# Batch 0 of a gated attention and mixer kernel: later score panels, pairwise side blocks, strips two outputs ahead and a later turn of z

## The chip, the cores and the metric

The kernel runs on one core of a Trainium2 chip. The metric is the device time of one execution in microseconds (us); the kernel before has a median of 1001.98 us over 5 runs (998.73 to 1006.83). Engines are named as in the profile: PE (matrix multiply; PEld is its weight load), DVE (vector), ACT (scalar, activations), POOL and SP. POOL and SP do almost nothing here but issue DMAs: POOL the loads and stores, SP the transposing DMAs.

## The reference

For each of 8 batches, with sequence length S = 3136, width 256 and z of width 64:

```
scores = z @ z.T / S                  # (S, S), symmetric
attn   = maximum(scores, 0) ** 2
x      = u * (attn @ v)
h      = (x.T @ U @ V).T              # low rank, 32
x2     = x + h
out    = x2 + maximum(x2 @ w1, 0) @ w2
```

This document is about the first two products in batch 0: the scores, and attn @ v.

## The kernel before

The sequence is cut into 25 tiles of 128 rows, called 0 to 24 (the last, 24, has 64 rows). Since the scores are symmetric, only one of the blocks (j, o) and (o, j) is computed. Panel j, the tile A[j], holds the 13 blocks (j, j) to (j, j+12), counted modulo 25. A score step (`score`, L292 to L314) makes up to 1024 columns of one panel, or a piece each of two: two PE matmuls into a pair of PSUM banks (L298, two such pairs exist), then ACT (relu and scale, L311) into A, then a square in place on DVE (L313). A whole panel of 13 blocks takes two such steps of 832 columns.

Output tile o is the sum over all 25 tiles j of block (j, o) times v[j] (`half`, L371: two matmuls per j on the two halves of the rows). For the 13 tiles j = o-12 to o the block is read from A[j]. For the other 12 the transposed blocks of panel o are needed: one transposing DMA from SP (`turn`, L331 to L334) writes them into a strip. A strip can be made only when the whole panel o is squared, and there are five strip buffers. Outputs are closed in pairs (`close_pair`, L385 to L395: ACT copy, DVE add, DVE multiply by u). Output 24 has 64 rows and works on quarters of the array (L405).

The outputs are taken in the order 12, 13, ..., 24, 0, ..., 11; position i in this order is output (12 + i) mod 25. The order of the instructions on every engine is written by hand: `manual_schedule` keeps program order on each engine, and `_spread` and `_merge` mix two lists of steps evenly.

In batch 0 nothing is there yet, so `start_up` works in groups of outputs. Outputs 12 to 15 are made first, then 16 to 19, which is where the change begins:

- The main part of 16 to 19 runs over pairs of panels; `make_stored` makes, for two panels at once, just the blocks that these four outputs need. Turns of panels 16 to 19 are behind it on SP. In the second and third round stood `double_z(1, ...)` (four DVE copies, L188) and `turn_z(1, ...)` (two transposing DMAs of SP, L195), which turn batch 1's z.
- The tail is the strip part of 16 to 19, merged with score steps: panels 20, 21 and 22 whole (`more`; two steps of panel 20 are taken already before), and the rest of the panels 15 down to 8, one step for each panel (`rest`), up to the panel's end.
- The main loop over i goes on with i = 8, output 20. `attend_steps` gives the 25 steps of an output, and `fill` the score steps spread among them: `first_at` says which panels and side blocks of batch 0 (side blocks are the first columns of panels 3 to 11) are made at which i, `next_at` those of batch 1. After each output, strips are turned four positions ahead: 21 and 22 are turned in the tail, 23 after output 20, 24 and 0 after 21, 1 after 22, and so on. `extend_z(1)` (a DVE copy of the turned z, L238) stands at i = 11. POOL loads two tiles of u for each pair of outputs and one part of v at i = 9, 11, 13, 15, 18 and 21.

From batch 1 on, the loop also has the mixer's matmuls of the batch before; nothing of that changes.

Of the kernel before, what the change touches and what calls it, by code (L numbers as in the profile page):

```python
# [42 lines left out]
def kernel(  # L43
# [31 lines left out]
    NG = 4  # L75
# [216 lines left out]
    def score(b, parts):  # L292

        ps = pair_psum()
        zT = zT_of(b)
        zT_flat = zT.rearrange("p t c -> p (t c)")
        for k, (j, c, n, _) in enumerate(parts):
            mm(  # L298
                out=ps[:, k, :n],
                lhsT=zT[halves[k], j, :],  # L300
                rhs=zT_flat[halves[k], c : c + n],
                start=True,
                stop=True,
            )
        if parts[0][3] is parts[-1][3]:
            n = parts[0][2]
            todo = [(parts[0][3], ps[:, :, :n] if len(parts) == 2 else ps[:, 0, :n])]
        else:
            todo = [(part[3], ps[:, k, : part[2]]) for k, part in enumerate(parts)]
        for dst, src in todo:  # L310
            nc.scalar.activation(out=dst, in_=src, func=AF.Relu, scale=sc)  # L311
        for dst, _ in todo:
            nc.vector.tensor_tensor(out=dst, in0=dst, in1=dst, op=ALU.mult)  # L313
# [345 lines left out]
    def beside(o, j, w, stop=(False, False)):  # L659
        t0, _ = pair_of(o)  # L660
        for h in range(1 if j == NF else 2):
            half(0, o, j, h, w, (t0, h) not in begun, stop[h], skip_group_check=True)
            begun.add((t0, h))

    def start_up():
        parts = ((8, 16), (0, 8), (16, NF))
        first_z(parts[:2])
# [89 lines left out]
                    if 0 <= o - j <= HALF:  # L757
                        beside(o, j, block(0, o, j))

        def make_stored(pair):  # L760
            todo = []
            for j in pair:
                k0, k1 = LEAD - j, min(NB, LEAD + NG - j)
                todo.append((j, LEAD * P, (k1 - k0) * P, A[j][:, k0 * P : k1 * P]))
            score(0, todo)

        nxt += [lambda pair=pair: make_stored(pair) for pair in pairs[:2]]
        run(nxt[:2])
        own = [
            lambda j=j, some=some: use_stored([j], some)  # L770
# [2 lines left out]
            if j <= some[-1]  # L773
        ]
        run(_merge(nxt[2:], own))
        rest = []
        for j in reversed(range(FIRST - NG, LEAD)):
            rest += score_steps(0, j, LEAD + NG - j, NB)
        more = [s for j in range(LEAD + NG, LEAD + 2 * NG - 1) for s in score_steps(0, j)]
        for i, pair in enumerate(pairs):  # L780
            if i + 2 < len(pairs):
                make_stored(pairs[i + 2])
            else:
                more.pop(0)()
            use_stored(pair, outs)
            if B > 1 and i in (1, 2):
                part = ((0, FIRST), (FIRST, NF))[i - 1]
                double_z(1, (part,))
                turn_z(1, (part,))
            if i == len(pairs) - 1:  # L790
                turn(0, LEAD + NG)
        tail = []
        for o in outs:
            js = [(o + 1 + i) % NT for i in range(HALF)]

            def close(o=o, j=js[-1]):
                beside(o, j, block(0, o, j), [o % 2 == 1] * 2)
                if o % 2:
                    close_pair(0, o)
                if o == outs[1]:  # L800
                    load_u(0, LEAD + NG)
                if o < outs[-2]:
                    turn(0, o + NG + 1)

            for i in range(3):
                some = js[4 * i : min(4 * i + 4, HALF - 1)]
                tail.append(lambda o=o, js=some: [beside(o, j, block(0, o, j)) for j in js])
            tail.append(close)
# [8 lines left out]
    for j, i in enumerate((6, 7, 8, 9, 3, 5, 4, 2, 9, 8, 7, 6)):  # L817
        own_at[i].append((j, 0, FIRST - j))

    first_at = {8: [(NT - 2, 0, NB), (0, 0, NB)], 9: [(NT - 1, 0, NB)], 10: [(1, 0, NB)]}  # L820
    first_at.update({11: [(2, 0, NB)], 12: []})
    for j, i in zip(range(3, FIRST), (10, 11, 11, 12, 12, 12, 12, 12, 12)):
        first_at[i].append((j, 0, FIRST - j))
    first_turns = {8: (NT - 2,), 9: (NT - 1, 0)}

    next_at = {i: [] for i in range(NT)}
    for j in range(FIRST):
        next_at[max(NB, FIRST + j)].append((j, FIRST - j, NB))
    for j, i in enumerate((14, 15, 16, 18, 19, 20, 24)):
        next_at[i].append((FIRST + j, 0, NB))  # L830

    def run(steps):
        for s in steps:
# [6 lines left out]
    for b in range(B):  # L840
# [104 lines left out]
```

## Time and profile before

| | |
|---|---|
| median of 5 runs | 1001.98 us (998.73 to 1006.83) |
| the profiled execution, its own time | 1004.27 us |
| its span, first to last instruction | 1002.5 us |
| mean granted TensorE clock | 0.998 |
| PE busy | 984.7 us, 98% |
| ACT busy | 612.6 us, 61% |
| DVE busy | 551.0 us, 55% |
| POOL busy | 171.6 us, 17% |
| turns of strips (SP) | 196 |

The profile is of one execution. A row of a group shows how many instructions it has, their mean duration, and the idle time of the engine ahead of them with what ended it. A PE that is "busy" need not be at its peak: a matmul of 256 columns is shown with about 270 ns from start to end, while the next can start about 54 ns after it. A window's row gives, for a stretch of time, each engine's busy us and the granted clock (1.00 is full speed). The chain of waits goes back from the last instruction to what released it, so it says which engine or DMA set the time at each moment. Waits of SP's queue, which the page does not list, are in an answer of their own.

### The profile page before, as it was taken

To read this page: it belongs to the slowest core of one execution; us is meant where nothing else is said; L and a number is where in the kernel's file an instruction comes from. 1 tells how busy PE (TensorE), PEld (TensorE's weight loads), DVE (VectorE), ACT (ScalarE), POOL (GpSimd) and SP (SyncE) were. 2 spreads that over 40 slices of the span, in tenths; PEclk is the share of its full clock that TensorE was granted. 3 is DMA by queue.
4 is the path that set the end of the run, shared out by engine and by line. 5 is a ranking of instruction groups with operands and counts; after the bars stand their busy time and mean duration, and the time that the engine had idled before them with its cause. 6 is when DMAs were issued, how large, how long until landed. Compare 5 with 4: busy or idle time off the path is not lost.

```text
span 1002.5 us, 31020 instructions
## 1 busy us (share of the span) xinstructions
PE 984.7 (98%) x13688; PEld 777.0 (78%) x13688; DVE 551.0 (55%) x1003; ACT 612.6 (61%) x835; POOL 171.6 (17%) x317
## 2 busy tenths in 40 slices
PE   8899999999999999999999999999999999999998
PEld 5578778787778878788787887778878788787866
DVE  6868754467544665446644566445664457542352
ACT  7877764667646776456764667556674666643154
POOL 5112112111121111221112211122111120011000
PEclk9999999999999999999999999999999999999999
DMA  9999989999899998999999997979989998678633
GB/s 192 185 188 201 179 152 181 193 178 173 149 171 184 175 157 175 186 181 171 162 177 171 182 170 149 186 167 179 173 149 194 168 190 157 123 147 164 128 95 101
DMA packets 414790, 167.94 MB, mean 168 GB/s; under 512 B 389488, under 2 KB 399408, under 8 KB 414656
## 3 DMA queue, kind: packets, MB, share of 16 engines
q1 hardware_dynamic: 385424, 99.68, 62.2%
q0 software_dynamic: 29232, 66.28, 29.0%
q8 instruction: 107, 1.75, 0.7%
q14 instruction: 27, 0.22, 0.1%
HBM read 61.88 MB, written 25.69 MB: 87 GB/s over the span
## 4 chain that ended last, share of the span: by engine, by line
PE 88%; DVE 4%; DMA 4%; ACT 3%; issue 1%; POOL 0%; DVEq 0%; POOLq 0%; ACTq 0%
PE ps L371 46%; PE ps L563 16%; PE ps L610 16%; PE ps L298 6%; ACT A L311 3%; DMA out_dram<-o_sb 2%; DVE A L313 1%; PE ps L405 1%; DMA strip<-A 1%; PE ps L531 1%; DVE x_bf L545 1%; DMA z_c<-in_z_dram 1%; PE ps L479 1%; DVE both L386 1%; DVE x_bf L395 0%
## 5 line engine op out<-in xcount | busy, mean ns | idle before, releaser
L311 ACT ACTIVATE A<-ps 128x832 bf16<-128x832 f32 (+9 forms) x477 | 359.1, 769 | 156.3 <-PE ps L298 147.5
L371 PE MATMUL ps<-v,A 64*128 64x256 bf16 x4988 | 341.8, 269 | 4.9 <-DVE o_sb L624 3.6
L313 DVE TENSOR_TENSOR A<-A 128x832 bf16<-128x832 bf16 (+9 forms) x477 | 244.6, 527 | 133.0 <-ACT A L311 129.8
L371 PE MATMUL ps<-v,strip 64*128 64x256 bf16 x4420 | 308.1, 270 | 2.8 <-DMA strip<-A 2.8
L371 PEld LDWEIGHTS <-A 64*128 64x128 bf16 x4988 | 246.5, 94 | 49.0 <-issue 13.5
L581 ACT ACTIVATE relu_bf<-ps 128x1024 bf16<-128x1024 f32 (+2 forms) x206 | 186.4, 912 | 140.0 <-PE ps L563 139.9
L371 PEld LDWEIGHTS <-strip 64*128 64x128 bf16 x4420 | 222.6, 94 | 37.2 <-DMA strip<-A 3.6
L624 DVE TENSOR_TENSOR o_sb<-ps,x_bf 128x512 f32<-128x512 f32 (+2 forms) x105 | 69.9, 665 | 248.4 <-PE ps L610 217.6
L610 PE MATMUL ps<-w_bf,relu_bf 128*128 128x256 bf16 (+1 forms) x1600 | 201.2, 273 | 0.0
L563 PE MATMUL ps<-ut,w_bf 128*128 128x512 bf16 (+2 forms) x896 | 198.6, 353 | 0.0
L610 PEld LDWEIGHTS <-relu_bf 128*128 128x128 bf16 (+1 forms) x1600 | 152.9, 98 | 45.6 <-issue 3.6
L563 PEld LDWEIGHTS <-w_bf 128*128 128x128 bf16 x896 | 84.8, 98 | 62.1 <-issue 6.9
L355 POOL DMA_DIRECT2D u_sb<-in_u_dram x96 | 53.8, 561 | 455.6 <-DVE x_bf L395 445.9
L298 PE MATMUL ps<-zT 64*128 64x416 bf16 (+8 forms) x812 | 131.6, 312 | 0.0
L385 ACT COPY both<-ps 128x512 f32<-128x512 f32 (+1 forms) x104 | 58.8, 566 | 75.9 <-PE ps L371 69.8
L637 POOL DMA_DIRECT2D out_dram<-o_sb x84 | 46.0, 547 | 281.1 <-DVE o_sb L624 277.8
L386 DVE TENSOR_TENSOR both<-ps,both 128x512 f32<-128x512 f32 (+1 forms) x104 | 69.3, 667 | 28.5 <-ACT both L385 28.0
L395 DVE TENSOR_TENSOR x_bf<-both,u_sb 128x512 bf16<-128x512 f32 (+1 forms) x104 | 69.8, 672 | 3.6
L545 DVE TENSOR_TENSOR x_bf<-ps,x_bf 128x512 bf16<-128x512 f32 (+1 forms) x112 | 65.5, 626 | 7.5 <-PE ps L531 7.4
L298 PEld LDWEIGHTS <-zT 64*128 64x128 bf16 x812 | 43.1, 94 | 4.0
L244 POOL DMA_DIRECT2D v<-in_v_dram x61 | 33.7, 554 | 0.8 <-DMA w_bf<-in_moe_w_ch_dram 0.7
L298 PE MATMUL ps<-relu_bf 64*128 64x416 bf16 (+9 forms) x121 | 22.2, 339 | 4.3 <-ACT A L311 3.2
(54 smaller groups left out, 206.3 us busy)
## 6 DMA issues: line engine op xcount, KB each, us to landing
u_sb<-in_u_dram POOLq DMA_DIRECT2D x96, 256.0 KB, 4.1
out_dram<-o_sb POOLq DMA_DIRECT2D x84, 256.0 KB, 3.2
v<-in_v_dram POOLq DMA_DIRECT2D x57, 192.0 KB, 4.7
strip<-A SPq DMA_TRANSPOSE x196, 5.4
out_dram<-o_sb SPq DMA_DIRECT2D x11, 256.0 KB, 2.0
z_c<-in_z_dram POOLq DMA_DIRECT2D x7, 384.0 KB, 5.7
u_sb<-in_u_dram POOLq DMA_DIRECT2D x16, 64.0 KB, 2.2
ut<-x_bf SPq DMA_TRANSPOSE x56, 3.8
```

Source lines behind the costliest of these rows:

```text
L298: mm(out=ps[:, k, :n], lhsT=zT[halves[k], j, :], rhs=zT_flat[halves[k], c : c + n], start=True, stop=True,)
L311: nc.scalar.activation(out=dst, in_=src, func=AF.Relu, scale=sc)
L313: nc.vector.tensor_tensor(out=dst, in0=dst, in1=dst, op=ALU.mult)
L371: mm(out=acc[t0][h][:, (o - t0) * D : (o - t0 + 1) * D], lhsT=w[halves[h]], rhs=v_both[b % 2][halves[h], j, :], start=start, stop=stop, **kw,)
L385: nc.scalar.copy(out=both[:, :w], in_=banks[1][:, :w])
L386: nc.vector.tensor_tensor(out=both[:, :w], in0=banks[0][:, :w], in1=both[:, :w], op=ALU.add)
L395: nc.vector.tensor_tensor(out=x_at(b, t0, n), in0=split(both[:, :w]), in1=u_sb[:, :n, :].rearrange("p t (a c) -> p t a c", c=P), op=ALU.mult,)
L545: nc.vector.tensor_tensor(out=q, in0=split(ps[h][:, : len(ks) * D]), in1=q, op=ALU.add)
L563: mm(out=ps[i][:, :w] if apart else ps[:, i, :w], lhsT=w1_bf[:, db, (hp + i) * P : (hp + i + 1) * P], rhs=uT[c][:, db, len(chunks[c]) * P ...
L581: nc.scalar.activation(out=relus[c][:, hp : hp + 2, :w], in_=ps[:, :, :w], func=AF.Relu)
L610: mm(out=ps[r, k * D : (k + 1) * D], lhsT=relus[c][:, ht, q : q + (TAIL if two else P)], rhs=w2_bf[:, ht, :], start=(ht < 1 + two), stop=( ...
L624: nc.vector.tensor_tensor(out=o_sb[:p].rearrange("p t (a c) -> p t a c", c=P), in0=split(ps[:p, k0 * D : (k + 1) * D]), in1=x_at(b, t, nk) ...
```

## The change

The change touches batch 0 (and the places where batch 1's first scores are made during batch 0):

- Panels 15 to 8 are no longer completed one by one. `make_stored` is now given the first output, and makes for pairs (15, 14), (13, 12), (11, 10), (9, 8) the blocks for outputs 20 to 23 in the tail. What is left of 15, 14 and of 13, 12 (ten blocks, for outputs 24 on) is made at i = 9 and i = 10.
- Panel 22 leaves the tail for i = 8. Panels 23, 24, 0, 1, 2 follow one for each output, at i = 9 to 13, and side blocks at 10 to 14.
- Strips are turned two outputs ahead: 21 in the tail, 22 after output 20, 23 after 21, 24 after 22, 0 after 23, 1 after 24, 2 and 3 after output 0, 4 and 5 after output 1; from then on four ahead as before.
- `double_z(1)` moves to i = 9, the two turns of z to i = 10 and i = 11, `extend_z(1)` to i = 12.
- Batch 1's first panels are made at i = 16, 17, 18, 20, 21, 22, 24 instead of 14, 15, 16, 18, 19, 20, 24, and its first side block at i = 14 instead of 13.

On SP's queue the two turns of z stood between strips 19 and 20; now the first stands between strips 23 and 24 and the second between 24 and 0. ACT and DVE have four more instructions each, PE eight fewer rows; POOL's order is the same.

```diff
+    def make_stored(pair, first, n=NG):
+        todo = []
+        for j in pair:
+            k0, k1 = first - j, min(NB, first + n - j)
+            todo.append((j, first * P, (k1 - k0) * P, A[j][:, k0 * P : k1 * P]))
+        score(0, todo)
...
-        rest = []
-        for j in reversed(range(FIRST - NG, LEAD)):
-            rest += score_steps(0, j, LEAD + NG - j, NB)
-        more = [s for j in range(LEAD + NG, LEAD + 2 * NG - 1) for s in score_steps(0, j)]
+        rest = [
+            lambda pair=pair: make_stored(pair, LEAD + NG)
+            for pair in zip(range(LEAD - 1, FIRST - NG, -2), range(LEAD - 2, FIRST - NG - 1, -2))
+        ]
+        more = [s for j in (LEAD + NG, LEAD + NG + 1) for s in score_steps(0, j)]
...
-            if B > 1 and i in (1, 2):
-                part = ((0, FIRST), (FIRST, NF))[i - 1]
-                double_z(1, (part,))
-                turn_z(1, (part,))
...
-                if o < outs[-2]:
-                    turn(0, o + NG + 1)
+                    turn(0, LEAD + NG + 1)
...
-    first_at = {8: [(NT - 2, 0, NB), (0, 0, NB)], 9: [(NT - 1, 0, NB)], 10: [(1, 0, NB)]}
-    first_at.update({11: [(2, 0, NB)], 12: []})
-    for j, i in zip(range(3, FIRST), (10, 11, 11, 12, 12, 12, 12, 12, 12)):
+    first_at = {8 + n: [(t, 0, NB)] for n, t in enumerate((22, 23, 24, 0, 1, 2))}
+    first_at[14] = []
+    for j, i in zip(range(3, FIRST), (10, 11, 12, 13, 14, 14, 14, 14, 14)):
         first_at[i].append((j, 0, FIRST - j))
-    first_turns = {8: (NT - 2,), 9: (NT - 1, 0)}
+    first_more = {9: (LEAD - 1, LEAD - 2), 10: (LEAD - 3, LEAD - 4)}
+    first_turns = {8: (22,), 9: (23,), 10: (24,), 11: (0,), 12: (1,), 13: (2, 3), 14: (4, 5)}
...
+    after_first = {i: [] for i in range(NT)}
+    for j in range(FIRST):
+        after_first[max(NB + 1, FIRST + j)].append((j, FIRST - j, NB))
+    for j, i in enumerate((16, 17, 18, 20, 21, 22, 24)):
+        after_first[i].append((FIRST + j, 0, NB))
...
+            if b == 0 and i in first_more:
+                fill.append(lambda pair=first_more[i]: make_stored(pair, LEAD + 2 * NG))
             if more:
-                fill += [s for key in next_at[i] for s in score_steps(b + 1, *key)]
+                coming = next_at if b else after_first
+                fill += [s for key in coming[i] for s in score_steps(b + 1, *key)]
...
-                if b and i == 7:
+                if b == 0 and i == 9:
+                    double_z(b + 1, ((FIRST, NF), (0, FIRST)))
+                if i == (7 if b else 10):
                     turn_z(b + 1, ((FIRST, NF),))
-                if b and i == 10:
+                if i == (10 if b else 11):
                     turn_z(b + 1, ((0, FIRST),))
...
-                if i == 11:
+                if i == (11 if b else 12):
                     extend_z(b + 1)
```

More of the change, by code (lines that the diff above doesn't have):

```diff
@@ L758, in use_stored @@
                         beside(o, j, block(0, o, j))
[L760 to L767, printed above, removed]
+        nxt += [lambda pair=pair: make_stored(pair, LEAD) for pair in pairs[:2]]
         run(nxt[:2])
@@ L775, in start_up @@
         run(_merge(nxt[2:], own))
-        rest = []
-        for j in reversed(range(FIRST - NG, LEAD)):
-            rest += score_steps(0, j, LEAD + NG - j, NB)
-        more = [s for j in range(LEAD + NG, LEAD + 2 * NG - 1) for s in score_steps(0, j)]
+        rest = [
[3 more added lines that the diff above has]
+        more = [s for j in (LEAD + NG, LEAD + NG + 1) for s in score_steps(0, j)]
         for i, pair in enumerate(pairs):
             if i + 2 < len(pairs):
-                make_stored(pairs[i + 2])
+                make_stored(pairs[i + 2], LEAD)
             else:
```

## The prediction, on record before the result

> **What bounds the kernel now.** I read the page's busy times and chain first, then the same sums by stage over the first 73 us (the rest of the order is untouched), then the chain, SP's queue and the waits there.
>
> ```profile
> PE 984.7 (98%) x13688; PEld 777.0 (78%) x13688; DVE 551.0 (55%) x1003; ACT 612.6 (61%) x835; POOL 171.6 (17%) x317
> ...
> PE 88%; DVE 4%; DMA 4%; ACT 3%; issue 1%; POOL 0%; DVEq 0%; POOLq 0%; ACTq 0%
> ```
>
> TensorE carries the run; what is not PE's own in the chain is 12%, part of it at the start. The change removes almost no PE work, so its gain can only be PE waiting, in the stages it touches. Busy us by stage (PE, weight load, DVE, ACT, POOL), then granted clock:
>
> ```profile
> 36.30:44.80 8.50, 7.83 (x115) 5.88 (x117) 6.41 (x12) 7.72 (x13) 0.54 (x1) 1.00 1.29 199
> 44.80:49.20 4.40, 2.05 (x39) 1.70 (x35) 3.36 (x9) 2.63 (x5) 1.07 (x2) 1.00 1.01 240
> 49.20:52.80 3.60, 3.60 (x34) 2.37 (x36) 0.59 (x1) 1.73 (x2) 0.00 (x0) 0.53 1.04 177
> 52.80:62.30 9.50, 9.50 (x164) 7.74 (x160) 6.55 (x12) 7.57 (x11) 1.62 (x3) 1.00 0.93 171
> 62.30:66.50 4.20, 3.64 (x63) 1.76 (x61) 3.94 (x8) 4.11 (x9) 1.03 (x2) 1.00 1.26 126
> 66.50:72.30 5.80, 5.80 (x108) 5.05 (x108) 3.39 (x11) 3.15 (x9) 1.61 (x3) 1.00 1.34 260
> ```
>
> The first row is the strip part of outputs 16 to 19, then come output 20 up to its strip, a stretch at half clock, outputs 20 to 23, output 24 (the short one), and 0 and 1 of batch 0. ACT is full in the first row and in output 24; PE waits in the second. The chain there (start, us, what) and PE's own timeline:
>
> ```profile
> 30.54 5.71 DMA strip<-A
> ...
> 37.88 2.85 ACT A L311 x4
> ...
> 42.95 6.20 DMA strip<-A
> 49.20 0.71 PE ps L371 x6
> ```
> ```profile
> 46.31 0.53 PE L371 MATMUL ps<-v,A 64*128 64x256 bf16 x6
> 49.20 0.71 PE L371 MATMUL ps<-v,strip 64*128 64x256 bf16 x6 [2.35 <-DMA strip<-A]
> ```
>
> PE has used its A blocks of output 20 and waits 2.35 us for strip 20, issued at 42.95. Panel 20's last ACT ends at 36.34. Why so late: SP's queue.
>
> ```profile
> 39.54 3.32 SPq L195 DMA_TRANSPOSE zT<-z_bf  x2
> 42.95 3.06 SPq L333 DMA_TRANSPOSE strip<-A  x1
> ```
>
> Both turns of batch 1's z stand in front of it.
>
> **Gains.** Unit prices from the chain after 68 us: 16 attention matmuls 0.87 us (0.0544 each), a score step of two 416-column matmuls 0.18. An 832-wide ACT takes 0.87, its DVE square 0.59.
>
> (1) Strip 20 takes z's place in SP's queue: issue 39.54, 3.4 us earlier. z's two turns there landed in 4.3 and 5.7 us; so strip 20 is there at 43.8 to 45.2. It is wanted at about 44.4. The wait of 2.35 goes; at most 0.8 of it stays.
>
> (2) The half clock goes with it: 3.6 us at 0.53 cost 3.6 x 0.47 = 1.7. The Trainium skill ("TensorE: Matmul & The Clock Gate", Part 1) puts the fall to half after an idle window of about 3.4 us; here an idle of 2.35 was enough, with the clock at 0.53 right behind it. By the rule new waits of 2 us would be free of it; by the row they may cost 1.7. I go by the row for waits of 2.3 and over.
>
> (3) Tail of outputs 16 to 19 (36.3 to 44.8). PE work: 92 matmuls 5.0 + score steps 1.7 = 6.7 of 8.5 us; 1.8 is lost to ACT, which runs its 12 panel pieces and 2 copies without a pause. Panel 22 (2 x 0.87) and ten blocks of panels 12 to 15 leave. ACT then has 2 x 0.87 + 5 x 0.65 + 0.50 + 0.38 + 0.28 + 2 x 0.59 = 7.3 raw; the old list is 10.0 raw in 8.65 us, so 7.3 takes 6.3. PE has 5.0 + 0.36 + 0.8 = 6.2, and strips 16 to 19 land as before (a wait of 0.4 for strip 17). The loss falls from 1.8 to 0.4: 1.4. Tail ends near 42.9.
>
> (4) Output 24, 62.3 to 66.5: 49 quarter matmuls take 1.33 us in every later batch, six score steps (1344 columns) 0.6; 2.3 of 4.2 is lost to ACT and to changing between the two kinds. Now three score steps stand there, panel 1's two and side 5: I leave 0.5. Gain 1.8.
>
> Sum: 2.35 + 1.7 + 1.4 + 1.8 = 7.2.
>
> **New waits.** Strips come two outputs ahead instead of four. Each output is 2.6 us of matmuls plus its score steps, about 3.2; a strip is wanted halfway into its output. So the lead from the turn to the need is 4.2 us for strip 22 (its panel is squared 0.8 after output 20 ends), 4.9 for 23, 4.2 for 24 (before the short output), 3.9 for 0, about 5 for 1. What a turn takes in this stretch, and over the whole run (min, median, max us from issue to landing):
>
> ```profile
> DMA to landing us min/median/max: 3.7/6.2/8.5
> ```
> ```profile
> DMA to landing us min/median/max: 3.6/5.4/10.4
> ```
>
> The skill's "DMA: Bandwidth & Descriptors", Latency and other measured facts, gives a transposing DMA 261 GB/s: 393 KB in 1.5 us, an estimate by which every lead is ample and the gain is all 7.2. The rows say 5.4 to 6.2, because copies (u 256 KB, v 192 KB) and earlier turns share the engines. I go by 5.4: in before this stretch carried a backlog of turns, which is gone in after.
>
> z's turns are not free where they now stand: the first is queued behind strip 23 and ahead of strip 24, the second ahead of strip 0; each holds SP 1.4 to 1.8 us. Late by: strip 22 0 (its queue is empty) to 1.2; strip 23 0.5; strip 24 5.4 + 1.5 - 4.2 = 2.7, less the 0.5 waited for 23, so 2.2; strip 0 then 5.4 + 1.5 - 3.9 - 2.2 = 0.8. Sum 3.5, between 1.0 (3.7 us a turn) and 13 (8.5 us a turn).
>
> A second new wait: the copy that extends z (L238) stands on DVE at output 24 and needs the second z turn, issued only about 55.5, landing near 61; before it found z landed. Behind it on DVE: the squares of panel 1 and side 5, then the closing of output 24; ACT's two copies L391 wait for that closing, and behind them stand panel 2's pieces, so PE runs out of score PSUM in output 0. ACT comes free near 61 + 0.55 + 1.18 + 0.63 + 0.42 = 63.8, by when PE, held by strips 24 and 0, is at about the same place: 0 beyond the strips' own, with bounds 0 and 1.6. If the strips are on time it is this that costs 1.6.
>
> Half clock for a gap of 2.2: 0 taken, 1.7 the other end.
>
> Free: the four z copies on DVE (1.9 us) at output 21, where DVE has 6.55 of 9.5 busy, cost panel 23's turn 0.6, inside the 0.5 to 1.2 above. Four more ACT and DVE pieces (0.3 to 0.65): ACT in output 22 has 4.2 against PE's 3.5; the two score PSUM pairs carry 1.7. Panels of batch 1 made two outputs later: at outputs 8 to 10 of the batch ACT gets a panel (1.7) beside a side (1.4) in about 3.3 us, hidden; bare, 0.3. POOL's order is unchanged, its loads follow the closings. Side blocks 7 to 11 all in output 1: six to eight small ACTs, 0.3.
>
> Net: 7.2 - 3.5 - 0.3 = 3.4. The profiled execution took 1004.27 around a span of 1002.5: span 999.1. It was 2.3 above the median, so from 1001.98: 998.6.
>
> **Rivals.**
> A. *Turns keep up.* With 3.7 us a turn, as one had in this stretch with an empty queue: late 1.0, and at most 0.6 of the DVE wait: gain 5.6 to 7.2, 995.5. For it: panels 22 on are turned singly, not in a burst. Against: u and v loads fall between them as before.
> B. *One wait for another.* Turns at 6.2, the stretch's median: 0.8 for 22, 1.0 for 23, 2.7 for 24, 0.8 for 0, one fall of the clock 1.7: 7.0. Gain about 0, 1002.
> C. *Slower: a two-output lead shorter than the DMA.* At 8.5 us a turn, the stretch's maximum: strip 22 late 4.3, 24 late 5.8, 1 late 3.3, two falls of the clock 3.4: 16.8 against 7.2, so 1011.5. It decides from about 6.3 us a turn. For it: in before the turns issued while a u and a v load were in flight took 7 to 8.5. Against: strip 24's queue holds one z turn and one short load.
>
> **How the numbers follow.** Forecast (gain 2 to 5.2) 0.45; A 0.25; B (-2.5 to 2) 0.16; C 0.14. 0.5% (5 us) is about what a measurement of this kernel tells from no change. Faster by more: A and a third of the forecast, 0.39. Slower by more: C, 0.14. Within: 0.47. The range from 994 (all 7.2, plus run to run) to 1004.5 (B's far end) leaves out C and the best edge of A, 0.2.
>
> **What would show it.** Step 1 and 2: no PE wait for a strip between 43 and 46, clock 1.00 throughout. Step 3: ACT with pauses in the tail, output 20 begins near 42.9. Step 4: quarter matmuls within 2.5 us. New waits: PE waits for strips at outputs 24 and 0, of 2.2 and 0.8; DVE waits for a DMA before L238. Batch 0's output 1 ends at 72.3 before, near 69 after. I am wrong if turns after 46 us take under 4 or over 7 us, or if PE falls to half clock again.

## The result, and the profile after

The changed kernel takes 1006.20 us in the median of 43 runs (1003.25 to 1012.98), beside 1002.61 for the kernel before in 80 runs (998.73 to 1010.82) on the same chips. The ratio is 1.0038, 95% interval 1.0029 to 1.0048: 3.8 us slower (the two medians lie 3.6 apart), certain in sign, and within the 0.5% that the prediction called no change. The forecast was 998.6 with a range up to 1004.5; the time lies above both.

The profiled execution of after took 1007.02 us, with a span of 1005.1 (before: 1004.27 and 1002.5). The page of after, the same two lines as shown of before:

```profile
PE 984.9 (98%) x13684; PEld 778.6 (77%) x13684; DVE 552.2 (55%) x1007; ACT 612.6 (61%) x839; POOL 171.1 (17%) x317
...
PE 87%; DMA 6%; DVE 4%; ACT 2%; issue 0%; POOL 0%; DVEq 0%; POOLq 0%; ACTq 0%
```

No engine has more work worth naming (DVE 1.2 us). In the chain, DMA went from 4% to 6% of the span, and ACT from 3% to 2%: TensorE waits for transfers instead of for ACT. By stage, with the columns as in the prediction (stretch, busy us of PE, weight load, DVE, ACT and POOL, granted clock, DMA share, GB/s), but cut where after's own outputs begin and end:

```profile
36.70:43.20 6.50, 6.46 (x109) 5.55 (x110) 4.12 (x8) 4.89 (x9) 0.00 (x0) 1.00 1.21 227
43.20:46.20 3.00, 2.86 (x46) 2.06 (x42) 2.96 (x9) 1.97 (x6) 0.54 (x1) 1.00 1.27 171
46.20:52.90 6.70, 5.86 (x98) 4.88 (x92) 5.82 (x13) 5.78 (x9) 1.07 (x2) 1.00 0.95 131
52.90:59.30 6.40, 5.62 (x92) 4.38 (x92) 3.09 (x8) 3.99 (x7) 1.62 (x3) 1.00 1.18 173
59.30:66.50 7.20, 3.29 (x48) 1.48 (x47) 2.73 (x5) 2.96 (x5) 1.08 (x2) 0.71 1.24 192
66.50:72.30 5.80, 5.80 (x77) 4.27 (x77) 4.39 (x10) 4.45 (x9) 1.09 (x2) 0.77 0.75 162
```

The tail of 16 to 19 (first row) is short and full of PE, output 20 is at its strip by 45.1, at full clock: the first half of the forecast came true. The row of output 24 (59.3 to 66.5) is where it is lost: PE is busy 3.29 of 7.20 us, and the clock falls there and in the row after. TensorE's timeline of after, where it begins on strips 20, 22, 24 and 2 (in brackets the idle time ahead):

```profile
45.14 0.83 PE L371 MATMUL ps<-v,strip 64*128 64x256 bf16 x12
...
53.68 0.72 PE L371 MATMUL ps<-v,strip 64*128 64x256 bf16 x10 [1.41 <-DMA strip<-A]
...
64.24 1.07 PE L405 MATMUL ps<-v,strip 64*64 64x256 bf16 x16 [3.91 <-DMA strip<-A]
...
77.78 0.28 PE L371 MATMUL ps<-v,strip 64*128 64x256 bf16 x2 [1.80 <-DMA strip<-A]
```

Strip 20 no longer makes it wait; 22, 24 and 2 do, 7.1 us together. The chain of after shows the same three as transfers (start, us, what):

```profile
38.88 6.22 DMA strip<-A
...
47.75 5.89 DMA strip<-A
...
55.38 8.81 DMA strip<-A
...
71.37 6.37 DMA strip<-A
```

SP's queue at the two turns ahead of output 24:

```profile
53.30 1.96 SPq L195 DMA_TRANSPOSE zT<-z_bf  x1
55.38 4.53 SPq L333 DMA_TRANSPOSE strip<-A  x1
```

Strip 24 is issued at 55.38 and wanted at 60.3, where PE has nothing else left: a lead of 4.9 us, against 8.8 from issue to landing. DVE at that place:

```profile
65.76 0.56 DVE L238 COPY zT<-zT 128x1536 bf16<-128x1536 bf16 x1 [4.12 <-DMA zT<-z_bf]
```

The extension of z stood 4.1 us for its turn, and everything behind it on DVE with it. The prediction had such a wait, but with its end near 61.

A useful ruler is the start of the multiply that closes each pair of outputs (L395), after minus before, in the profiled runs: -0.9 and -1.2 us at (16,17) and (18,19), **-5.4 at (20,21)**, -3.5 at (22,23), +0.8 at 24, **+5.2 at (0,1)**, +5.4 at the end of batch 0 and until 263 us. So the change is 5.4 us ahead there, and between 52 and 80 us loses nearly 11. Some 0.6 of the 5.4 is score work that it only puts off past output 21 (an estimate from the matmul columns of L298 made by then, at 0.0544 us for 256: 8.4 us before, 7.8 after); by the end of batch 0 both have made the same. It ends at +2.6, mostly because two PE waits of 2.0 and 1.7 us for DVE's work in the mixer at 283 and 649 us, in before's profiled run, do not recur in after's; nothing of the change is near them, and the median of many runs is the better size.

The clock can be followed without profiles, since every run lists its mean. In 92 of the 201 runs of before beside the experiments it was 1.000, and its mean was 0.9988; in 2 of 44 of after it was 1.000, mean 0.9973. That is 1.2 and 2.7 us lost (1003 times what is missing), so up to 1.5 of the 3.8 us are half clock; what of it lies in a wait, when PE stands anyway, costs nothing.

### The profile page after: what moved, and what is told of

It reads as the page before. It is cut to its first block, busy times and chain, and to the rows that moved or that the text cites. A ratio compares the mean times of both kernels' runs of the same rounds, so it can differ in the third digit from the quotient of the medians.

```text
span 1005.1 us, 31018 instructions
## 1 busy us (share of the span) xinstructions
PE 984.9 (98%) x13684; PEld 778.6 (77%) x13684; DVE 552.2 (55%) x1007; ACT 612.6 (61%) x839; POOL 171.1 (17%) x317
## 4 chain that ended last, share of the span: by engine, by line
PE 87%; DMA 6%; DVE 4%; ACT 2%; issue 0%; POOL 0%; DVEq 0%; POOLq 0%; ACTq 0%
PE ps L371 45%; PE ps L563 17%; PE ps L610 17%; PE ps L298 6%; DMA strip<-A 4%; ACT A L311 2%; PE ps L405 1%; DVE A L313 1%; PE ps L531 1%; DVE x_bf L545 1%; DMA out_dram<-o_sb 1%; DMA z_c<-in_z_dram 1%; PE ps L479 1%; DMA zT<-z_bf 0%; DVE both L386 0%
## 5 line engine op out<-in xcount | busy, mean ns | idle before, releaser
L311 ACT ACTIVATE A<-ps 128x832 bf16<-128x832 f32 (+10 forms) x481 | 359.5, 764 | 160.4 <-PE ps L298 146.5
L313 DVE TENSOR_TENSOR A<-A 128x832 bf16<-128x832 bf16 (+10 forms) x481 | 245.4, 524 | 133.4 <-ACT A L311 130.4
L371 PEld LDWEIGHTS <-A 64*128 64x128 bf16 x4988 | 248.2, 94 | 45.1 <-issue 10.1
L298 PE MATMUL ps<-zT 64*128 64x416 bf16 (+8 forms) x812 | 131.9, 312 | 0.8 <-ACT A L311 0.8
L395 DVE TENSOR_TENSOR x_bf<-both,u_sb 128x512 bf16<-128x512 f32 (+1 forms) x104 | 69.8, 671 | 3.6
L298 PEld LDWEIGHTS <-zT 64*128 64x128 bf16 x812 | 43.5, 94 | 4.7 <-issue 1.0
L298 PE MATMUL ps<-relu_bf 64*128 64x416 bf16 (+9 forms) x117 | 23.2, 344 | 3.1 <-ACT A L311 2.4
```

Of the source, the lines that this page charges most:

```text
L298: mm(out=ps[:, k, :n], lhsT=zT[halves[k], j, :], rhs=zT_flat[halves[k], c : c + n], start=True, stop=True,)
L371: mm(out=acc[t0][h][:, (o - t0) * D : (o - t0 + 1) * D], lhsT=w[halves[h]], rhs=v_both[b % 2][halves[h], j, :], start=start, stop=stop, **kw,)
L395: nc.vector.tensor_tensor(out=x_at(b, t0, n), in0=split(both[:, :w]), in1=u_sb[:, :n, :].rearrange("p t (a c) -> p t a c", c=P), op=ALU.mult,)
```

## Experiments

All were timed against before; the ratios have 95% intervals. "At (20,21)" and so on is the ruler above against before, in the profiled run. A profiled run can lie several us from its kernel's median, so it says which wait came, and the ratio says what it is worth.

### Is it z's turns in front of strips 24 and 0?

**z right behind strip 21.** After, with both turns of z in the gap where SP has nothing to do (42.7 to 47.7 us in after), and the doubling at its old place.

```diff
+            if B > 1 and i in (1, 2):
+                double_z(1, (((0, FIRST), (FIRST, NF))[i - 1],))
...
+                    if B > 1:
+                        turn_z(1, ((FIRST, NF), (0, FIRST)))
...
```

> The changed kernel with one thing moved: the four copies that double z go back to where they stood in the kernel before, and the two turns of z are issued right behind strip 21, where SP stands idle for 5 us (42.7 to 47.8) in the changed kernel. Theory Z (the two turns of z in front of strips 24 and 0 made the wait of 3.9 us and the half clock behind it): the wait at output 24 falls under 1 us, the clock stays at 1.00, about 7 us less than the changed kernel, so some 3 us faster than before (ratio 0.996 to 0.998). Theory L (two outputs of lead are too short for any strip): strip 24 still comes 2 us or more late, ratio 1.001 to 1.004. Theory V (the v load among the strips): the same as L here.

Measured 1.0076 (1.0053 to 1.0098). Strip 22, now behind z, took 9.6 us, a v load beside it 9.5. Its TensorE timeline:

```profile
57.02 0.82 PE L371 MATMUL ps<-v,strip 64*128 64x256 bf16 x6 [5.38 <-DMA strip<-A]
```

The theory that the idle gap takes z's turns for nothing falls: the wait moved to strip 22 and grew. -6.0 at (20,21), +7.7 at the end of batch 0.

**z as before.** After, with doubling and turns back at their old place; the rest of the change stays.

```diff
+            if B > 1 and i in (1, 2):
+                part = ((0, FIRST), (FIRST, NF))[i - 1]
+                double_z(1, (part,))
+                turn_z(1, (part,))
...
```

> The changed kernel with doubling and turns of z where they stood before (in front of strip 20), so only the panels, the pairwise side blocks and the two-output lead are left of the change. Theory Z: strip 20 comes late as before (a wait of 2 to 4 us with the half clock, since output 20 begins 1.5 us earlier), strips 24 and 0 nearly in time: ratio 1.000 to 1.003. Theory L: strip 20 late and strips 22, 24, 2 late as well: 1.004 to 1.010.

Measured 1.0100 (1.0064 to 1.0136). Strip 20 late by 3.6 us (with 6.8 us of half clock), 22 by 2.0, 2 by 1.8, and strip 24 by 3.0: it took 8.1 us with no turn of z near it. z is not what makes 24 late, so that theory (Z) falls. Moving z later is the good part of the change: it makes after 0.6% faster than this kernel.

**z alone.** Before, with only z's doubling, turns and extension, and with them batch 1's first scores, moved as in the change.

```diff
-                double_z(1, (part,))
-                turn_z(1, (part,))
...
+                if b == 0 and i == 9:
+                    double_z(b + 1, ((FIRST, NF), (0, FIRST)))
+                if i == (7 if b else 10):
                     turn_z(b + 1, ((FIRST, NF),))
...
-                if i == 11:
+                if i == (11 if b else 12):
                     extend_z(b + 1)
```

> The kernel before with z alone moved, as the change moves it (doubling at i = 9, turns at i = 10 and 11, extension at 12, batch 1's first panels two outputs later); panels, side blocks and strips four ahead as before. The prediction's steps 1 and 2 say: strip 20 is no longer waited for (2.35 us) and the half clock goes (1.7 us), 4 us faster. Theory L: strips four ahead have room for z's turns, so the ratio is 0.995 to 0.997. Theory Z: z's turns delay strips here too, but these have two outputs more of lead; 0.996 to 0.999.

Measured 1.0022 (1.0005 to 1.0039). Strip 20's wait and the half clock are gone, -4.6 at (20,21), -3.7 at (22,23), and then +4.4 at output 24. Its waits from 60 to 80 us (engine, line, what for, us in total, times, longest):

```profile
ACT both L391 <- DVE both L386: 8.6, 1, 8.6
DVE zT L238 <- DMA zT<-z_bf: 7.6, 1, 7.6
...
PE ps L298 <- DMA zT<-z_bf: 2.8, 1, 2.8
...
PE ps L298 <- ACT A L311: 2.4, 2, 1.9
```

With four strips of lead no strip is late by more than 0.6 us here. The extension of z waits 7.6 us for its turn and blocks DVE, DVE blocks ACT, ACT blocks the scores. Steps 1 and 2 of the prediction are confirmed by themselves. So is the block that it priced at 0, or at 1.6 with the strips in time: here it costs more.

**z behind strip 22.** Before, with only z's turns later: three strips later, where the change puts them four and five strips later.

```diff
-                turn_z(1, (part,))
+                double_z(1, (((0, FIRST), (FIRST, NF))[i - 1],))
...
+                    if B > 1 and o == outs[1]:
+                        turn_z(1, ((FIRST, NF), (0, FIRST)))
...
```

> The kernel before with one thing moved: the two turns of z go behind strip 22 instead of in front of strip 20 (doubling, extension, panels and strips four ahead as before). In the run with z alone moved, SP stood idle there from 44.0 to 47.9. Theory P (the prediction's steps 1 and 2: z in front of strip 20 costs the wait and the half clock, 4.1 us, and what z costs later comes from its late landing alone): strip 20 in time, z landed near 52, no wait of the extension: 3 to 4.5 us faster, ratio 0.9955 to 0.997. Theory N (any gap that is closed there comes back at outputs 24 to 1, where turns and loads are the limit): ratio 0.999 to 1.002.

Measured 1.0085 (1.0057 to 1.0114): -4.8 at (20,21), then strip 23 took 9.3 us, PE waited 4.6; +6.3. **The same with pairwise side blocks:**

```diff
+        rest = [
+            lambda pair=pair: make_stored(pair, LEAD + NG)
+            for pair in zip(range(LEAD - 1, FIRST - NG, -2), range(LEAD - 2, FIRST - NG - 1, -2))
+        ]
...
+    first_more = {9: (LEAD - 1, LEAD - 2), 10: (LEAD - 3, LEAD - 4)}
...
```

> The kernel with z's turns behind strip 22 and, besides, the pairwise side blocks (ten blocks of panels 12 to 15 made at i = 9 and 10 instead of in the tail); panels and strips four ahead as before. By the prediction's step 3, the part of it that the ten blocks are (about 1.0 of 10.0 us of ACT work in the tail): 0.5 to 1 us less than the run with z behind strip 22 alone. If ACT has no room at i = 9 and 10: the same or 0.5 us more.

Measured 1.0037 (1.0019 to 1.0056), so the pairs are worth 0.5%, with intervals that only just do not meet; the profiles show 0.2 to 0.7 us of that in the tail, and the wait for strip 23 at 3.2 instead of 4.6. A strip with both of z's turns right in front of it is late in all three kernels: strip 22, turned two outputs ahead, and here strip 23, which before turns three ahead.

### Is it the loads among the turns?

**Batch 1's v later.** After, the four loads of i = 9 to 15 moved behind the startup.

```diff
-        v_at = dict(zip((9, 11, 13, 15, 18, 21), V_PARTS[3:]))
+        v_at = dict(zip((16, 17, 18, 19, 20, 21), V_PARTS[3:]))
```

> The changed kernel with the loads of batch 1's v from i = 9, 11, 13, 15 put off to i = 16 to 21; nothing else. Theory V (the loads of v, mixed with turns, stretch a turn to 8 us and more): turns between 46 and 66 us take 4 to 5 us, the wait of 3.9 us at output 24 falls under 1.5, about 5 us less than the changed kernel (ratio to before 0.998). Theories Z and L: the wait at output 24 stays at 2.5 us or more, ratio 1.002 to 1.004.

Measured 1.0088 (1.0057 to 1.0120). Where the loads left, it did what was hoped: z's first turn took 4.7 instead of 8.3 us, strip 24 4.3 instead of 8.8, the wait at 24 was gone (strip 0 came 1.0 late), and (22,23) and 24 stood at -5.6 and -4.1. With the loads in a burst, turns then took 8 to 12 us, and batch 0 ended at +4.8.

**One load earlier.** After, only the load of i = 11 moved to 8.

```diff
-        v_at = dict(zip((9, 11, 13, 15, 18, 21), V_PARTS[3:]))
+        v_at = {8: (4,), 9: (3,), 13: (5,), 15: (6,), 18: (7,), 21: (8,)}
...
```

> The changed kernel with one load moved: the 192 KB of batch 1's v that stood at i = 11 go to i = 8, where the DMA engines have no turn from 46.4 to 49.9 us. Theory M (turns and loads in flight together move about 135 GB/s where turns alone move 265: that stretch, 55 to 61 us, makes strip 24 late): the wait of 3.9 us at output 24 falls under 2 and the half clock goes, 3 to 5 us less than the changed kernel, ratio to before 0.998 to 1.001. If the two-output lead alone is at fault, whatever is mixed: unchanged, 1.003 to 1.005.

Measured 1.0040 (1.0025 to 1.0056, 5 runs), no different from after; the gain that theory M named did not come. In its profile z's turn and strip 24 took 4.2 us each, and no wait at 24 is left. The window of 53 to 59 us, of this kernel and then of after:

```profile
53.00:59.00 6.00, 4.53 (x79) 4.21 (x81) 3.04 (x9) 3.76 (x7) 1.05 (x2) 1.00 1.13 242
```
```profile
53.00:59.00 6.00, 5.32 (x90) 4.29 (x90) 2.99 (x8) 3.59 (x7) 1.53 (x3) 1.00 1.18 173
```

At the same DMA share (1.13 and 1.18) the engines move 242 GB/s against 173. Strip 22 is late by 1.6 and strip 0 by 0.9, and PE loses 1.7 behind the extension, with half clock after it.

The same split runs through all profiles in which z's first turn stands where the change puts it. In the eight with a v load beside it, that turn and the strip behind it took 6.0 to 8.3 and 5.4 to 8.8 us (after has the slowest of each); in the six where that load is gone or stands elsewhere, 4.2 to 5.4 and 3.8 to 5.6.

**No loads at all.** Before and after without the six loads of batch 1's v in batch 0; that part of batch 1's v is zeros, so batch 1's attn @ v is not computed from it.

```diff
+            nc.gpsimd.memset(v_both[1][:, V_PARTS[3][0] :, :], 0.0)
...
-                if b == 0 and i in v_at:
-                    load_v(b + 1, v_at[i])
...
```

> The kernel before without the six loads of batch 1's v that stand among the outputs of batch 0 (1.1 MB); POOL writes zeros there once, early, so that part of batch 1's attn @ v is left out. Theory T (from 30 to 106 us the DMA engines are the limit, turns and loads together): less to move and nothing mixed in, 2 to 5 us faster than the kernel before, ratio 0.995 to 0.998. If only the order of the turns matters: 0.998 to 1.000.

> The changed kernel without the same six loads (the same part of batch 1 left out). Theory T: the gain of the first 52 us (5.4 us at outputs 20 and 21) is kept, since the turns find room: faster than the kernel before without them, ratio to before 0.991 to 0.996, and waits for strips 22, 24 and 2 together under 3 us. Theory L (two outputs of lead are too short with or without loads): as slow as the changed kernel, 1.001 to 1.004.

Measured 0.9993 (0.9979 to 1.0007) for before without them, 1.0001 (0.9982 to 1.0019) for after. So the same six loads cost before nothing that shows, and after 3.7 us by the ratios (its intervals with and without them do not meet; the ends nearest each other leave 1.0). Still, after without loads is no faster than before. In its profiled run, which at 1007.76 us was its slowest, it holds -6.0 at (20,21), and is back at -0.4 by the end of batch 0, with strips 22, 0 and 2 late by 0.9, 0.8 and 1.6, and 1.7 us lost behind the extension. Theory T, by which the total of transferred bytes sets the end of the startup, had called for 4 to 9 us: fewer bytes do not keep the gain.

### Is it the extension of z, blocking DVE?

**Extension at i = 15.** After, with that copy alone moved.

```diff
-                if i == (11 if b else 12):
+                if i == (11 if b else 15):
                     extend_z(b + 1)
```

> The changed kernel with the extension of z (the copy on DVE) at i = 15 instead of 12; nothing else. Theory D (the copy that waits for the second turn of z blocks DVE, and behind it ACT, so that panel 2 and strip 2 come late): the wait of 1.8 us for strip 2 and ACT's 1.2 us behind the closing of output 24 go, 1.5 to 2.5 us less than the changed kernel (ratio to before 1.001 to 1.003). If the extension only waits beside the strips: the same as the changed kernel, 1.003 to 1.005.

Measured 1.0030 (1.0006 to 1.0055), against 1.0038 for after: not to be told apart. DVE's wait is gone from the profile; strips 22 and 2 are late by 1.6 and 2.3, each with half clock behind. **With the loads of v spread to 14 to 23 as well:**

```diff
-        v_at = dict(zip((9, 11, 13, 15, 18, 21), V_PARTS[3:]))
+        v_at = dict(zip((14, 16, 18, 20, 22, 23), V_PARTS[3:]))
```

> The changed kernel with the extension of z at i = 15 and batch 1's v loads at i = 14, 16, 18, 20, 22 and 23 instead of 9, 11, 13, 15, 18 and 21. In the run with all of v at 16 to 21 the outputs up to 1 came 1.5 us ahead of before, and the burst of loads then cost 5 us. Theory V with D: the early wait at output 24 stays under 1 us, no burst follows: 2 to 4 us faster than before, ratio 0.996 to 0.999. If loads cost the same wherever they stand: 1.003 to 1.006.

1.0042 (1.0015 to 1.0068): the 2 to 4 us of theories V and D did not come; in its profile strip 2 is late by 2.5, and turns take 8.2 and 10.8 us beside the loads at 75 to 85 us. **With three of the loads at i = 8 instead:**

```diff
-        v_at = dict(zip((9, 11, 13, 15, 18, 21), V_PARTS[3:]))
+        v_at = {8: (3, 4, 5), 15: (6,), 18: (7,), 21: (8,)}
...
```

> The changed kernel with the v loads of i = 9, 11 and 13 all at i = 8 and the extension of z at i = 15. Theory M: no load of v among the turns 23 to 1, waits at outputs 22, 24 and 2 together under 2 us (7.1 in the changed kernel), 5 to 7 us less than the changed kernel, ratio 0.995 to 0.999. If three loads at once delay strip 22 instead: a wait of 2 to 4 us at output 22, ratio 1.000 to 1.003.

1.0013 (1.0000 to 1.0026), better than after (the intervals do not meet): block and loads together are worth 0.25%. Strips 22 and 2 are still late, by 2.1 and 2.2.

**z alone, extension at 15,** and batch 1's first side blocks from i = 16 on:

```diff
+        after_first[max(NB + 3, FIRST + j)].append((j, FIRST - j, NB))
...
-                if i == 11:
+                if i == (11 if b else 15):
...
```

> The kernel before with z alone moved later, as in the run with z alone, but the extension of z at i = 15 and batch 1's first side blocks from i = 16. In that run outputs 20 to 23 were 3.7 to 4.6 us ahead of before, and all of it went at the extension (7.6 us of DVE, 8.6 us of ACT behind it) and at the first use of z. Theory E (that extension and first use were the whole loss): no such wait, 3 to 4.5 us faster than before, ratio 0.9955 to 0.9975. Theory M: strips or loads give back 2 us or more, 0.998 to 1.002.

1.0042 (1.0028 to 1.0057). The 3.7 us are kept up to (0,1), then ACT waits 2.8 for a strip's turn and PE 2.7 for ACT, with half clock; +3.1. Theory E's 3 to 4.5 us did not come: the loss is not bound to one place.

### Is it the lead?

**Three ahead.** After, with panel 22 back in the tail and strips turned three outputs ahead.

```diff
-        more = [s for j in (LEAD + NG, LEAD + NG + 1) for s in score_steps(0, j)]
+        more = [s for j in (LEAD + NG, LEAD + NG + 1, LEAD + NG + 2) for s in score_steps(0, j)]
...
-    first_turns = {8: (22,), 9: (23,), 10: (24,), 11: (0,), 12: (1,), 13: (2, 3), 14: (4, 5)}
+    first_turns = {8: (23,), 9: (24,), 10: (0,), 11: (1,), 12: (2,), 13: (3,), 14: (4, 5)}
...
```

> The changed kernel with panel 22 back in the tail and strips turned three outputs ahead (22 in the tail, 23 after output 20, and so on); all else as changed. Theory G (the turns' queue stands idle for 5 us, 42.7 to 47.8, because panel 22 comes after the tail, and that DMA time is missing later): the queue runs on in the tail, the wait of 1.4 us at output 22 goes and the one at output 24 falls from 3.9 to about 2; ACT takes back 1 us of the tail; 2 to 4 us less than the changed kernel, ratio 0.999 to 1.002. Theory M alone: the wait moves to whichever strip stands beside the loads, ratio 1.002 to 1.006.

Measured 1.0026 (1.0008 to 1.0044), against 1.0038 for after: not to be told apart. Strip 22 is in time. Its waits from 60 to 75 us:

```profile
ACT both L391 <- DVE both L386: 7.3, 1, 7.3
DVE zT L238 <- DMA zT<-z_bf: 5.8, 1, 5.8
...
PE ps L298 <- ACT A L311: 4.8, 1, 4.8
```

Now PE is ahead far enough for the extension to hurt in full: 4.8 us. **Three ahead and the extension at 15:**

```diff
-                if i == (11 if b else 12):
+                if i == (11 if b else 15):
```

> The same three-ahead kernel with the extension of z at i = 15, v loads where the change has them. Theory D (the copy that waits for z on DVE blocks ACT and PE): the 4.8 us at output 0 and the half clock go, 3 to 5 us less than the run three ahead, ratio to before 0.998 to 1.000. Theory T: the time comes back at later strips, 1.001 to 1.003.

1.0003 (0.9981 to 1.0025), not to be told from three ahead alone. The 4.8 us are gone, and -4.8 at (20,21) is still -3.7 at (0,1). Then, from 60 to 90 us:

```profile
ACT A L311 <- DMA strip<-A: 5.6, 2, 3.9
...
PE ps L298 <- ACT A L311: 1.6, 2, 1.2
```

ACT is to write batch 1's first side block into a panel whose strip is still being read by its turn, and stands 3.9 us. After has the same wait (3.2 us at 77.8). **These side blocks one or two outputs later too:**

```diff
-        after_first[max(NB + 1, FIRST + j)].append((j, FIRST - j, NB))
+        after_first[max(NB + 3, min(NT - 1, FIRST + j + 1))].append((j, FIRST - j, NB))
```

> The three-ahead kernel with the extension of z at i = 15 and, besides, batch 1's side blocks one to two outputs later. In that kernel's run ACT waited 5.6 us for turns that still read the panel that batch 1's side block overwrites, and PE 1.2 us behind ACT with a half clock after it. Theory W (that write behind the turn is where the last 3 us of the gain go): no such ACT wait, ratio to before 0.996 to 0.998. If the strips then come late instead: 0.999 to 1.002.

0.9996 (0.9974 to 1.0018), 1000.91 us: the best kernel of the study, 0.42% below after with intervals that do not meet, and not to be told from before: theory W's 0.996 to 0.998 did not come. Its waits from 43 to 106 us:

```profile
PE ps L371 <- DMA strip<-A: 3.6, 3, 1.5
```

ACT and DVE wait for no DMA any more; three strips are late, none by over 1.5, and no half clock. It holds -4.7 at (0,1) and -2.0 at the end of batch 0.

**The same, but two ahead** (and panel 22 at i = 8, as in after):

```diff
-    first_turns = {8: (23,), 9: (24,), 10: (0,), 11: (1,), 12: (2,), 13: (3,), 14: (4, 5)}
+    first_turns = {8: (22,), 9: (23,), 10: (24,), 11: (0,), 12: (1,), 13: (2, 3), 14: (4, 5)}
```

> The changed kernel (strips two ahead, v loads where it has them) with the extension of z at i = 15 and the same later side blocks of batch 1: only the lead is left of the suspected costs, so this against the run three ahead is the lead alone. Theory L: waits for strips 22, 24 and 2 stay at 4 us or more, 2 to 4 us slower than three ahead, ratio to before 1.000 to 1.003. If the lead costs nothing: the same as three ahead within 1 us.

1.0069 (1.0041 to 1.0097). From 43 to 106 us:

```profile
PE ps L371 <- DMA strip<-A: 4.2, 2, 2.5
```

The lead alone, with panel 22's place that goes with it, makes 0.73% here, about 7 us, and the intervals do not meet. But this is the largest of four pairs of kernels here that differ by the lead alone: after against three ahead makes 0.12%, both with the extension at 15 makes 0.27%, and both with three v loads at i = 8 as well (the kernel below) 0.04%, each with intervals that meet. At the end of batch 0 the profiled runs differ by 3.2, 0.2, 1.7 and 0.6 us in these four. So two outputs are nowhere better than three, and a price of 7 us is not settled. This kernel's 8 runs lie wide (1003.41 to 1014.25 us; the profiled one took 1005.52), and that it is no faster, if anything slower, than the kernel with only the extension moved (1.0030) is not explained: the intervals overlap by 0.14%.

**Three ahead, extension at 15, three v loads at i = 8** (side blocks as in after):

```diff
-        v_at = dict(zip((9, 11, 13, 15, 18, 21), V_PARTS[3:]))
+        v_at = {8: (3, 4, 5), 15: (6,), 18: (7,), 21: (8,)}
...
```

> The changed kernel with panel 22 back in the tail and strips three ahead, the extension of z at i = 15, and the v loads of i = 9, 11 and 13 at i = 8. It puts together what each cost by itself: the wait for strip 22 (2.1 us and a half clock of 1.7 in the run with v early), the block on DVE and ACT (4.8 us and 1.7 in the run three ahead). If these causes add: 3 to 5 us less than either, ratio to before 0.996 to 0.999. If the DMA engines' total sets the end of batch 0 whatever the order (theory T): 1.000 to 1.003.

1.0009 (0.9991 to 1.0027): loads put early at three ahead bring nothing beyond the extension's move. In its profile they stand right behind the turn of strip 22, which takes 13.7 us and is late by 4.3.

## Why the prediction was wrong

**Right.** The bound was read rightly: PE with its waits in the stretch from 36 to 73 us. Step 1: strip 20 was issued at 38.9, there at 45.1, no wait (predicted 43.8 to 45.2). Step 2: no half clock there, though over many runs of before it is worth 1.2 us, not the 1.7 of its one profile. Step 3: output 20 begins at 43.0 to 43.2 (predicted 42.9). Together -5.4 us at (20,21), where the prediction's first three steps gave 2.35 + 1.7 + 1.4 = 5.45; that they agree so closely is luck in part, since 0.6 of the 5.4 is work put off. The leads were right as well: 4.5 us for strip 22 and 4.9 for strip 24, where 4.2 was put for each. The list of what would show it wrong had it: turns of over 7 us after 46, and PE at half clock again.

**Step 4** holds as far as it can be seen: output 24 takes 7.1 us (59.4 to 66.5), 3.9 of it the wait, and 2.3 of the rest at half clock, which would be 1.1 at full clock if PE set the pace there. That leaves about 2 of its own, against a forecast of 2.4.

**The step that failed is "New waits"**, and in it the time of a turn: "I go by 5.4: in before this stretch carried a backlog of turns, which is gone in after." The turns from strip 22 to strip 2, z's two among them, took 5.9, 8.3, 8.8, 5.8, 5.7, 3.7 and 6.4 us (strip 23's landing is not in the trace): 6.4 in the mean, over the 6.3 from which rival C was to decide. In place of 3.5 us of waits there were 1.4 at strip 22 (said: 0 to 1.2), 3.9 at 24 (2.2) and 1.8 at 2 (not forecast; the sum stopped at strip 1). The half clock was taken as 0, with 1.7 as the other end; by the clock's records it lasted from 62.3 to 69.1, and the 4.9 us of it behind the wait cost 2.4. Together 9.5, and 0.8 for a wait behind ACT at 94.7 us, against a gain of 7.2: 3.1 slower. This is near the 3.8 of the ratio, but in part by luck, since it counts the gains of steps 3 and 4 in full (below). The backlog was not the cause of slow turns: they were slowest where only three stood in SP's queue (8.3 and 8.8 us), and the v load beside them goes with the slow ones (5.4 to 8.8 us in the eight profiles with it, 3.8 to 5.6 in the six without; after with that one load moved had 4.2). How slow differs from kernel to kernel: with the same queue and the same load, the two took 6.0 and 5.4 us in the kernel with side blocks later and two ahead. What else sets it is open. The mechanism of C was right, and its places 22 and 24 too, at well under its price of 16.8.

**Steps 3 and 4 by the end of batch 0.** The windows from 36 us to the last closing of batch 0, of before, of after, and of the best kernel (three ahead, side blocks later):

```profile
36.00:105.00 69.00, 65.13 (x1081) 52.42 (x1083) 49.55 (x95) 51.39 (x77) 11.07 (x18) 0.98 1.17 200
```
```profile
36.00:110.40 74.40, 65.40 (x1079) 54.43 (x1080) 52.09 (x104) 51.94 (x81) 10.61 (x18) 0.95 1.09 187
```
```profile
36.00:103.00 67.00, 63.07 (x1084) 52.11 (x1085) 51.71 (x103) 52.03 (x81) 11.16 (x18) 1.00 1.24 205
```

PE is idle for 3.9, 9.0 and 3.9 us of them. Half clock while PE works costs 1.7, 2.4 and 0; what is left of the busy time is 63.4, 63.0 and 63.1 us. So after's 5.4 us of loss are 5.1 of idle PE and 0.7 of half clock, less 0.4. The 3.2 us that steps 3 and 4 were to bring are mostly gone by then: 0.4 in the busy time, and 0.4 in the idle time outside the waits named here (1.5 before, 1.1 after). The likely reason is that the score work which they take from the tail and from output 24 has to be made behind them: a gain at the place it left was counted as a gain of the batch. The best kernel is ahead of before by little more than the half clock.

**The rule and the row.** For turns, the 261 GB/s of the Trainium skill ("DMA: Bandwidth & Descriptors", Latency and other measured facts) is about what they reach alone: after moved 267 GB/s from 37.0 to 39.5 us. From 55 to 61, with a v load and two turns in flight, it moved 137. Neither that rule nor the median of the run (5.4) held for the mixture; the rows of turns with loads in flight, 7 to 8.5, noted under C and not used, came near it. For the clock, after's gap of 3.9 us cannot tell the skill's window of about 3.4 us ("TensorE: Matmul & The Clock Gate", Part 1) from the row, but the clock fell 2.0 us into it, and it fell with 10 of the 14 gaps of 2.05 to 2.9 us that the runs hold (last section): the row was the better guide. The forecast gap of 2.2 was just under the line drawn at 2.3 and got no price.

**A slip in the chances.** A forecast of 2 to 5.2 us cannot put a third of its chance beyond 5 us. With almost all of it inside, faster by more is about 0.25 to 0.28 and within about 0.6.

**DVE behind the extension of z** was taken as 0, "bounds 0 and 1.6". In after it is hidden behind strip 24, as said. But PE stands 4.8 us behind it as soon as the strips are in time (three ahead): the upper bound was too low, since DVE's wait was taken to end near 61, and in after it ended at 65.8. Moving it in that kernel took the ratio from 1.0026 to 1.0003, with intervals that overlap. That ACT waits to overwrite a panel which a turn still reads was missed altogether: 3.2 us at 77.8, and the closing of (0,1) stands behind it: +5.2, where PE itself is at +2.1 at 73 us and, behind strip 2's wait, at +3.9.

**What is shown, and what is not.** Shown by intervals that do not meet: v's loads cost after 1.0 us or more, 3.7 by the ratios, and before nothing that shows; moving z later is worth 0.6% within the change; the lead of two outputs costs something in one of four pairs, and in the other three nothing that can be told. Only read from profiles: which strip is late in which kernel, since the place moves with each edit. No kernel here beats before. Those with z's turns moved are 3.7 to 6.6 us ahead at output 21, and the best of them ends batch 0 only 2.0 ahead, 1.7 of it the half clock, and is not to be told from before in the ratio. Taking away loads, blocks and late strips one at a time brought out the next wait each time. Why PE's idle time never came under before's 3.9 us is open.

## What to carry to other kernels

A wait that is removed in front of a stretch fed by transfers that are made just in time can go to the next transfer, as it did here: compare the lead of each with what it takes beside everything else in flight there, at its slow end and not at its median. When a DMA is put later, list every in-order engine that has an instruction waiting for it, or waiting to overwrite what it reads (here z's copy on DVE, a panel's rewrite on ACT), and price what is queued behind as if the engines ahead were in time. Work that is moved out of a full stretch is a gain only if the stretch that takes it has room: add up to a point where both orders have made the same work. And put a stretch of half clock (3.4 us, so 1.7) on each gap of over 2 us: 20 of the 24 such gaps here had one, and it costs nearly as much as the gap.

## What the runs showed of the hardware

**Turns often stop for about 1.3 us just after an instruction fetch.** The page of after, in its list of DMA queues (packets, us, share), has

```profile
q8 instruction: 107, 1.75, 0.7%
```

One such packet comes every 6 to 13 us in batch 0. Of the 62 stretches in after's trace in which turn packets take over 1 us, 53 begin within 1.5 us behind one, and of 59 in before 52; by chance it would be about one in six (107 times 1.5 us in 1005). Two such stretches of after, from its windows:

```profile
50.90:52.20 1.30, 1.08 (x17) 0.73 (x12) 1.14 (x3) 1.30 (x3) 0.00 (x0) 1.00 0.44 13
75.90:77.20 1.30, 0.08 (x2) 0.00 (x0) 0.00 (x0) 0.00 (x0) 0.00 (x0) 1.00 1.27 20
```

The last two columns: in the second, DMA engines are as "busy" as anywhere (1.27) and move 20 GB/s, where turns alone move 267; PE stands. Strips 22, 24 and 2 each met one while in flight, some 4.1 us in all by an estimate (1.3, 1.3, and 1.5 from 62.5 to 64.0, where 36 GB/s were moved), beside the 7.1 us that PE waited for them. This is a coincidence in time; no kernel here removed a fetch, so that it is the cause was not tried.

**Half clock has no sharp threshold here.** Over the profiled runs of before, after and all the experiments, it came with all 10 PE gaps of over 2.9 us (up to 5.4), 10 of 14 between 2.05 and 2.9, and 3 of 18 between 1.5 and 2.05; once it came with a gap of 1.2. In the long gaps it can begin inside the gap. It lasts 3.4 or 6.8 us, so a gap that sets it off may cost as much again: 1.7 us and more.
